# Gated delta rule and cosine feed-forward on one core: the first pair's triangular blocks inverted by doubling on TensorE, and a new order of all work

## The chip, the cores and the metric

One Trainium2 chip, one of its cores. The metric is the time of one execution in microseconds on the device, as the median over runs. The kernel's five engines are TensorE (PE), VectorE (DVE), ScalarE (ACT), GpSimd (POOL) and SyncE (SP); each takes its own instructions in the order in which they were issued to it, and they wait for each other through semaphores. Transfers are issued from SP and ACT.

## What is computed

Two blocks, one behind the other. The first is a delta-rule attention over 768 time steps for 4 batches and 8 heads of 48; the second a feed-forward block whose activation is h cos(h).

```python
k_n = k / (np.linalg.norm(k, axis=-1, keepdims=True) + 1e-06)
state = np.zeros((B, H, D, D))
for t in range(S):
    kt, vt, bt = (k_n[:, :, t], v[:, :, t], beta[:, :, t, None])
    y[:, :, t] = np.einsum('bhd,bhde->bhe', q[:, :, t], state)
    v_old = np.einsum('bhde,bhd->bhe', state, kt)
    state = state + bt[:, :, :, None] * np.einsum('bhd,bhe->bhde', kt, vt - v_old)
...
x = attn_out.transpose(0, 2, 1, 3).reshape(B * S, H * D)   # 3072 x 384
h = x @ w_in                                               # 384 x 2048
out = (h * np.cos(h)) @ w_out                              # 2048 x 384
```

## The kernel before

**Tiles.** The 768 steps are cut into 24 units of 32. The four batches lie side by side on the 128 partitions, 32 steps each. Two units make a pair, and a pair of units gives 256 tokens for the feed-forward block; there are 12 pairs.

**A unit.** k, q and v are loaded and k and q turned by PE (`turn`, L592, `turn_out`, L602). `gram` (L625) multiplies k with k and q; `gram_keys` (L636) scales the key part by beta and by the norms of k (a power on POOL, L544, task `norms`, and five small DVE operations, task `scale`), and `gram_queries` (L659) masks the other. Within a unit the recurrence is a unit lower triangular 32x32 system for each batch and head. Its matrix I + N, with N strictly triangular, is inverted once, and the unit is finished by matmuls: `state` (L795, what the state so far gives), `right` (L812), `solve` (L861 or L867, the inverse times the right side), `solve_out` (L879), `update` and `update_out` (L892, L900, the new state), `within` and `within_out` (L909, L922), and `features` (L930), which turns the result for the feed-forward block.

**The inverse of a pair** goes through memory, so that 128 partitions each hold half the rows of one of the 64 blocks of 32x32: `gram_put` writes the scaled key products, `gram_get` reads them back in the other layout (L698), `eye` puts an identity (L714), `inv` in seven pieces runs over the columns, two operations each (a product into `part`, L735, and a difference, L742), `put` writes the inverse (L756), and `get` reads it for each unit (L775). For pairs 1 to 11 this is done on POOL.

**Pair 0** is different (`HALVED = 1`). `fold` (L648 to L653) keeps the two 16x16 blocks on the diagonal and sets the block below them aside. The 16x16 blocks go the same way through memory, 15 columns, on DVE, in a bank of PSUM. Each unit of this pair then takes three steps of matmuls instead of one: `solve_half` (p_w, L825, with the half inverses), `between` (p_v, L825, with the block set aside, L845 taking the difference), and `solve`.

**The feed-forward block.** w_in and w_out come as pairs of 32-bit words, 12 and 16 transfers (`weights`, L487), and are made into 32-bit floats in three steps: `split` on ACT (L495, L497), `shift` on DVE (L501, L506) and `add` on POOL (L510). For pairs 0 and 1 `hidden(p, f)` (L951) multiplies features by w_in, 24 records of matmuls each; `hidden(0, 0)` needs blocks 0 to 2 of w_in, `hidden(0, 2)` 0 to 5, `hidden(0, 4)` 0 to 8 and `hidden(0, 6)` all 12. `turns`, `rest`, `cos` and `gate` make h cos(h) on ACT and DVE. `out` (L1148) multiplies by w_out; `out(0, 0, k)` needs its first 4k + 4 blocks. From pair 2 on the first product is made in 20 products of sums (`layer`, L1125, with `x_sum`, L1040, on DVE or POOL), and from pair 1 on the second in 7 (L1205, with `left` sums, L1221, on DVE or POOL).

**The order.** Every piece of work is a task with a key such as `('gram', 3)`. A table `LINE` lists all tasks in one order, found beforehand by a search; they are emitted in that order, so it fixes each engine's queue, and all transfers of SP and ACT are also held in that one order. A set `OTHER` names the tasks that take the other of two engines: ACT instead of SP for a transfer, POOL instead of DVE (or the reverse, for `x_sum`) for a sum.

Of the kernel before, what the change touches and what calls it, by code (L numbers as in the profile page):

```python
# [10 lines left out]
FP = mybir.dt.float32  # L11
# [5 lines left out]
C = 32  # L17
# [7 lines left out]
def _consts():  # L25
# [14 lines left out]
            p[:, None] // 16 % 2 == np.arange(2)[None, :],  # L40
# [6 lines left out]

class Order:

    OTHER = {  # L50
        ('gram_put', 0), ('put', 0), ('get', 1), ('k', 2), ('gram_put', 2), ('q', 3), ('v',
        3), ('gram_get', 1), ('k', 5), ('k', 6), ('gram_put', 6), ('get', 6), ('v', 7),
        ('gram_put', 7), ('blocks', 8, 1), ('blocks', 9, 1), ('gram_put', 9), ('blocks', 11,
        1), ('put', 5), ('get', 11), ('blocks', 12, 1), ('gram_put', 12), ('blocks', 13, 1),
        ('put', 6), ('get', 14), ('put', 7), ('v', 16), ('blocks', 16, 0), ('get', 17),
        ('k', 18), ('v', 18), ('put', 9), ('k', 20), ('gram_get', 10), ('gram_put', 22),
        ('blocks', 23, 1), ('store', 0, 1), ('right', 4, 4), ('right', 3, 4), ('left', 1, 1,
        1), ('left', 1, 4, 0), ('in_sums', 20), ('x_sum', 2, 'd'), ('x_sum', 2, 'n'),
        ('x_sum', 2, 'm'), ('x_sum', 2, 'e'), ('x_sum', 2, 'k'), ('x_sum', 2, 'g'),
        ('x_sum', 2, 'l'), ('x_sum', 2, 'f'), ('left', 2, 1, 0), ('left', 2, 2, 0), ('left',  # L60
        2, 4, 0), ('store', 2, 0), ('x_sum', 3, 'd'), ('x_sum', 3, 'n'), ('x_sum', 3, 'e'),
        ('x_sum', 3, 'k'), ('x_sum', 3, 'g'), ('x_sum', 3, 'i'), ('x_sum', 3, 'l'),
        ('x_sum', 3, 'f'), ('x_sum', 3, 'h'), ('x_sum', 3, 'b0'), ('left', 3, 2, 0),
        ('left', 3, 3, 0), ('x_sum', 4, 'd'), ('x_sum', 4, 'n'), ('x_sum', 4, 'm'),
        ('x_sum', 4, 'e'), ('x_sum', 4, 'g'), ('x_sum', 4, 'f'), ('x_sum', 4, 'h'),
        ('x_sum', 4, 'b0'), ('left', 4, 1, 0), ('left', 4, 2, 0), ('left', 4, 1, 1),
        ('store', 4, 1), ('x_sum', 5, 'd'), ('x_sum', 5, 'n'), ('x_sum', 5, 'm'), ('x_sum',
# [156 lines left out]
def kernel(  # L224
# [99 lines left out]
    nc.vector.memset(bq, 0.0)  # L324


    HALVED, HC = 1, C // 2
    off_blocks, half_zt = [], []
    eye16 = early[:, EYE : EYE + HC * HC].rearrange("p (r i) -> p r i", i=HC)
    half_tiles = [  # L330
# [1445 lines left out]
```

## Time and profile before

| | |
|---|---|
| median of 3 runs | 653.76 us (650.46, 653.76, 655.24) |
| the profiled execution: time, span | 656.46 us, 654.7 us |
| PE busy | 594.1 us (91%) |
| DVE, ACT, POOL busy | 504.0 (77%), 295.2 (45%), 457.0 (70%) |
| moved by transfers | 51.52 MB in 215,628 packets |
| granted TensorE clock, mean | 0.998 |
| chain that ended last | PE 72%, POOL 8%, DMA 8%, DVE 4%, issue 3% |

The span is the time from the first to the last instruction that the profile shows; the time of the execution is 1.8 us longer. The chain that ended last is followed back from the last instruction, at each step to what released it. A row of groups gives a line of the kernel, engine, operation, tiles and sizes, the number of records, their busy time and mean, and the idle time before them with what ended it.

### The profile page before, as it was taken

What the parts mean: (1) busy time and instruction counts of PE and PEld (TensorE: products, weight loads), DVE (VectorE), ACT (ScalarE), POOL (GpSimd) and SP (SyncE); (2) the same over time, 40 slices, a digit from 0 to 9 for tenths busy, and PEclk for the clock granted to TensorE, in tenths of its full rate; (3) what the DMA queues carried; (4) which work ended last, traced back from release to release, by engine and by line L of the source; (5) the groups of instructions that cost most, each with busy time, mean ns of one, the idle gap of its engine ahead of it and who ended that gap; (6) DMA issues with size and microseconds to landing.
All of it is one profiled execution on the core that took longest, in us unless ns stands there. A gap on an engine that the chain in (4) does not pass through costs nothing.

```text
span 654.7 us, 23397 instructions
## 1 busy us (share of the span) xinstructions
PE 594.1 (91%) x9784; PEld 555.2 (85%) x9784; DVE 504.0 (77%) x1035; ACT 295.2 (45%) x518; POOL 457.0 (70%) x813
## 2 busy tenths in 40 slices
PE   3315689999999999999999999999899999999996
PEld 3204689897899999998999999999898999999996
DVE  4684487899899987987879879889668778666581
ACT  2533365663234454634634535536334545545340
POOL 4368868978888778887788788748687388424130
PEclk9999999999999999999999999999999999999999
DMA  8886576462373363454352631441541300300000
GB/s 167 193 192 151 132 178 143 92 135 48 62 125 57 53 114 57 87 80 74 71 85 43 110 53 41 67 90 22 97 69 26 82 12 3 58 2 25 1 24 25
DMA packets 215628, 51.52 MB, mean 79 GB/s; under 512 B 207076, under 2 KB 210420, under 8 KB 215524
## 3 DMA queue, kind: packets, MB, share of 16 engines
q1 hardware_dynamic: 160168, 35.06, 28.0%
q10 hardware_dynamic: 55100, 14.53, 11.1%
q8 instruction: 77, 1.26, 0.8%
q0 software_dynamic: 256, 0.45, 0.3%
q14 instruction: 27, 0.22, 0.1%
HBM read 39.24 MB, written 10.75 MB: 76 GB/s over the span
## 4 chain that ended last, share of the span: by engine, by line
PE 72%; POOL 8%; DMA 8%; DVE 4%; issue 3%; ACTq 2%; ACT 1%; SPq 1%; POOLq 0%; DVEq 0%
PE p_out L1205 25%; PE p_h L1125 23%; PE p_h L951 7%; PE p_out L1148 3%; POOL z L742 3%; POOL part L735 3%; PE p_kq L795 3%; PE p_u L867 2%; PE p_s L892 2%; DMA gb<-g_dr 2%; PE p_kq L909 2%; DMA kp<-in_k_dram 2%; PE p_g L625 2%; PE p_h L1205 1%; PE p_z L930 1%
## 5 line engine op out<-in xcount | busy, mean ns | idle before, releaser
L735 POOL TENSOR_TENSOR part<-z,gb 128x126 f32<-128x126 f32 (+22 forms) x341 | 149.5, 439 | 53.8 <-DMA gb<-g_dr 17.7
L742 POOL TENSOR_TENSOR z<-z,part 128x126 f32<-128x126 f32 (+22 forms) x341 | 154.7, 454 | 26.7
L1205 PE MATMUL p_out<-w_out,g_ffn 128*128 128x192 f32 x672 | 121.7, 328 | 3.1 <-ACT o L1244 2.0
L1205 PEld LDWEIGHTS p_out<-w_out,g_ffn 128*128 128x128 f32 x672 | 107.8, 190 | 4.5 <-ACT o L1244 2.2
L1004 ACT ACTIVATE turns<-turns,halfpi 128x512 f32<-128x512 f32 x96 | 68.3, 720 | 82.2 <-DVE turns L995 72.1
L1205 PE MATMUL p_out<-w_sum,g_ffn 128*128 128x192 f32 x496 | 91.1, 330 | 1.4 <-DVE o L1257 1.4
L1125 PE MATMUL p_h<-x_sum,w_in 128*128 128x128 f32 x640 | 83.3, 278 | 0.2
L1205 PEld LDWEIGHTS p_out<-w_sum,g_ffn 128*128 128x128 f32 x496 | 79.4, 190 | 2.8 <-DVE o L1257 1.6
L1125 PEld LDWEIGHTS p_h<-x_sum,w_in 128*128 128x128 f32 x640 | 77.5, 191 | 1.9 <-ACT p_h L1137 0.4
L988 ACT ACTIVATE turns<-g_ffn,quarter_turn 128x512 int32<-128x512 f32 x70 | 49.6, 718 | 50.8 <-DVE g_ffn L1142 18.0
L1142 DVE TENSOR_TENSOR g_ffn<-g_ffn,p_h 128x512 f32<-128x512 f32 x80 | 54.0, 681 | 16.1 <-PE p_h L1125 15.0
L1007 DVE TENSOR_TENSOR g_ffn<-turns,g_ffn 128x512 f32<-128x512 f32 x70 | 52.0, 751 | 14.0 <-ACT turns L1004 13.7
L922 ACT COPY y<-p_kq 32x384 f32<-32x384 f32 x96 | 45.2, 470 | 36.2 <-PE p_kq L909 31.2
L995 DVE SCALAR_TENSOR_TENSOR turns<-g_ffn,turns 128x512 f32<-128x512 f32 x70 | 54.1, 781 | 7.5 <-ACT turns L988 7.3
L1125 PE MATMUL p_h<-x_sum,in_sum 128*128 128x128 f32 x400 | 53.8, 278 | 0.3 <-POOL x_sum L1040 0.2
L1125 PEld LDWEIGHTS p_h<-x_sum,in_sum 128*128 128x128 f32 x400 | 49.6, 191 | 1.7 <-POOL x_sum L1040 0.7
L951 PE MATMUL p_h<-x_ffn,w_in 128*128 128x128 f32 x384 | 48.2, 284 | 0.2 <-issue 0.2
L1221 POOL TENSOR_TENSOR g_ffn<-g_ffn 128x512 f32<-128x512 f32 x21 | 29.9, 1426 | 25.8 <-DVE g_ffn L1007 15.6
L951 PEld LDWEIGHTS p_h<-x_ffn,w_in 128*128 128x128 f32 x384 | 45.9, 198 | 1.4 <-issue 0.3
L544 POOL TENSOR_TENSOR knrm<-ksum,halves 128x16 f32<-128x16 f32 (+1 forms) x14 | 37.9, 2709 | 12.3 <-DVE ksum L532 12.1
L1257 DVE SCALAR_TENSOR_TENSOR o<-p_out,o 128x192 f32<-128x192 f32 x74 | 25.0, 351 | 27.3 <-PE p_out L1205 26.7
L1125 PE MATMUL p_h<-x_ffn,w_in 128*128 128x128 f32 x320 | 42.3, 276 | 0.0
(135 smaller groups left out, 1020.6 us busy)
## 6 DMA issues: line engine op xcount, KB each, us to landing
gb<-g_dr SPq DMA_DIRECT2D x18, 256.0 KB
g_ffn<-in_moe_w_out_dram SPq DMA_DIRECT2D x11, 384.0 KB
vp<-in_v_dram SPq DMA_DIRECT2D x80, 48.0 KB
g_ffn<-in_moe_w_in_dram SPq DMA_DIRECT2D x6, 512.0 KB
g_ffn<-in_moe_w_in_dram ACTq DMA_DIRECT2D x6, 512.0 KB
kp<-in_k_dram SPq DMA_DIRECT2D x112, 24.0 KB
out_dram<-o SPq DMA_DIRECT2D x14, 192.0 KB
zt<-z_dr SPq DMA_DIRECT2D x72, 32.0 KB
```

Of the source, the lines that this page charges most:

```text
L544: nc.gpsimd.tensor_tensor(out=scales[m][2][:, part], in0=sums[m, part.start][:, 0:n], in1=halves[:, 0:n], op=ALU.pow,)
L735: eng.tensor_tensor(out=part, in0=z[:, 0:rows, j, None].to_broadcast(shape), in1=a[:, j, None, j + 1 :].to_broadcast(shape), op=ALU.mult,)
L742: eng.tensor_tensor(out=behind, in0=behind, in1=part, op=ALU.subtract)
L922: nc.scalar.copy(by_parity(y[quarter(b)]), p_kq[quarter(b ^ 1), :, b % 2])
L951: nc.tensor.matmul(p_h[:, i], w_in[:, t, (4 * k + i) * 128 : (4 * k + i + 1) * 128], xts[p][:, t, unit * 128 : (unit + 1) * 128], start=(i ...
L988: nc.scalar.activation(turns[p, f], hidden_of(p, f), AF.Identity, bias=quarter_turn, scale=TURN)
L995: nc.vector.scalar_tensor_tensor(out=r, in0=hidden_of(p, f), scalar=TURN, in1=t, op0=ALU.mult, op1=ALU.subtract,)
L1004: nc.scalar.activation(r, r, AF.Sin, bias=halfpi, scale=2.0 * math.pi)
L1007: nc.vector.tensor_tensor(out=place(p, f), in0=step_of(rests.pop((p, f)), f), in1=step_of(hidden_of(p, f), f), op=ALU.mult,)
L1125: nc.tensor.matmul(p_h[:, e], in_block(*w)[:, e], x_of(p, b), start=new and e == 0, stop=True, skip_group_check=True,)
L1142: nc.vector.tensor_tensor(out=part_of(p, to), in0=part_of(p, one), in1=part_of(p, two), op=op)
L1205: nc.tensor.matmul(p_o, left(p, part, a)[:, e % 4], right(e, b), start=(e == 0), stop=(e == FT // 2 - 1), skip_group_check=True,)
```

## The change

Pair 0 no longer goes through memory. For its two units N is kept in place, four blocks of 32x32 on the partitions and eight heads side by side, and the inverse is made by matmuls of 32x32 blocks. First the two 16x16 blocks on the diagonal: with M their N, (I - M)(I + M^2)(I + M^4)(I + M^8) is built in four levels, of which the first squares M, the next two square and multiply at once, and the fourth only multiplies; each also carries the transpose that the next one needs as its stationary side. The last two levels put in the block below the diagonal: OFF times the inverse, then the inverse times that, which is subtracted. Each level is done for even and odd heads by themselves (`par`). The matmuls write a bank of PSUM of those that `hidden` uses; ACT copies what the next level needs, DVE makes the sums, and DVE transposes once. The powers lie in the tiles `in_sum` (unit 0) and `w_sum` (unit 1), which the feed-forward block uses later. The folds, `solve_half`, `between` and the choice of engine for `inv` are gone, and both units of pair 0 take one `solve`.

```diff
-    HALVED, HC = 1, C // 2
+    DOUBLED = 2
...
+    masks_dr = nc.inline_tensor(_masks(), name="masks")
+    masks = in_sum.rearrange("p a b c -> p (a b c)")[:, MASKS : MASKS + 3 * C]
+    nc.gpsimd.dma_start(out=masks, in_=masks_dr.ap())
+    near_block, far_block, eye32 = (masks[:, i * C : i * C + C] for i in range(3))
...
+    def double_first(n):
+        masked(n, N_T, near_block)
+        m = power(n)
+        nc.vector.transpose(m[:, N1], m[:, N_T])
+
+    def double_rest(n):
+        m = power(n)
+        nc.vector.tensor_tensor(
+            out=m[:, Y0], in0=eye32[:, None, :].to_broadcast([128, H, C]), in1=m[:, N_T],
+            op=ALU.subtract,
+        )
+        masked(n, OFF, far_block)
+        gs.pop(n)
+
+    LEVELS = [
+        [(0, N_T, slice(N1, N1 + 1)), (1, N1, slice(N_T, N_T + 1))],
+        [(1, P2, slice(P2_T, Y0 + 1)), (0, P2_T, slice(P2, P2 + 1))],
+        [(0, P4, slice(Y1, Y1 + 1)), (1, P4_T, slice(P4, P4 + 1))],
+        [(0, P8, slice(Y2, Y2 + 1))],
+        [(0, OFF, slice(Y3_T, Y3_T + 1))],
+        [(0, MIX_T, slice(Y3, Y3 + 1))],
+    ]
...
+    def double(n, level, par):
+        m = power(n)
+        p = p_ds[n, par] = h_bank("p_d", n, level, par).rearrange(
+            "p x (j i) -> p x j i", i=C
+        )
+        for at, one, two in LEVELS[level]:
+            for j in range(NP):
+                for b in range(B):
+                    nc.tensor.matmul(
+                        p[quarter(b), at : at + two.stop - two.start, j],
+                        m[quarter(b), one, 2 * j + par],
+                        m[quarter(b), two, 2 * j + par],
+                    )
+
+    def double_copy(n, level, par):
+        to, at = COPIES[level]
+        nc.scalar.copy(power(n)[:, to, par::2], p_ds[n, par][:, at])
+
+    def double_add(n, level, par):
+        m = power(n)
+        to, one, at = ADDS[level]
+        nc.vector.tensor_tensor(
+            out=m[:, to, par::2], in0=m[:, one, par::2], in1=p_ds[n, par][:, at],
+            op=ALU.subtract if level == 5 else ALU.add,
+        )
+
+    def double_turn(n, par):
+        m = power(n)
+        nc.vector.transpose(m[:, Y3_T, par::2], m[:, Y3, par::2])
...
     def solve(n):
-        zt, rhs = zts.pop(n), rhss.pop(n)
+        zt, rhs = power(n)[:, WHOLE] if n < DOUBLED else zts.pop(n), rhss.pop(n)
```

In the declaration of the tasks, the sums of `in_sum` now also wait for `solve` of both units, and the loads of k and v no longer wait for `gram_get` of pair 0. `LINE` and `OTHER` are wholly new. Read out by name, the transfers and POOL's work begin so (`w` is `weights`; the first loads of k, q, beta and constants stand ahead in both):

```text
transfers before: w0 k2 w1 k3 w2 q2 gram_put0 gram_put1 w3 q3 w4 gram_get0 v0 k4 w5 v1 w6
  gram_put2 w7 k5 gram_put3 put0 gram_get1 w8 q4 w9 get0 w10 k6 w11 get1 w12 q5 v2 w13 ...
transfers after:  w0 k2 q2 w1 k3 w2 q3 k4 w3 v0 w4 k5 gram_put2 w5 gram_put3 q4 w6 gram_get1
  v1 w7 k6 w8 v2 w9 w10 q5 k7 v3 w11 w12 k8 w13 q6 w14 gram_put4 gram_put5 w15 w16 put1 get2 ...
POOL before: norms norms norms norms add2 clear add0 add3 add5 add4 add1 norms add6 add7 inv1(3 of 7)
  add9 add8 inv1(2) add10 inv1(2) add12 add11 add13 add15 add17 norms inv2 ...
POOL after:  norms norms norms clear add0 norms add2 add3 add1 norms add4 add5 inv1(4) add6 inv1(3)
  add8 add10 add7 norms add9 add12 add11 add13 add14 add15 inv2(4) add17 add19 inv2(1)
  add16 add18 add20 inv2(2) add21 ...
```

On PE, the new order has turn(2), gram(1), turn(3), gram(2), gram(3) and turn(4) between the levels of the doubling; turn(5) ahead of features(0); and behind it the last two levels of unit 1, gram(4), hidden(0, 0), solve(1), update(1), hidden(0, 2). Of ACT's work, split(5) and split(6) stand between the copies of the later levels, and split(9) ahead of within_out(0). Of DVE's, weigh(0), which needs v of unit 1, stands ahead of the transposes of even heads of unit 0. Over the whole kernel 28 of the 110 `x_sum` operations move from DVE to POOL, and four `left` sums and one sum of w_out from POOL to DVE. The last three stores of the last pair stand together at the very end; before, one of them did.

## What the change was predicted to do

> **What bounds the kernel now.** The busy tenths of the page come first (40 slices of 16.4 us).
>
> ```profile
> PE   3315689999999999999999999999899999999996
> POOL 4368868978888778887788788748687388424130
> DMA  8886576462373363454352631441541300300000
> ```
>
> TensorE (PE) is full from the seventh slice to the end; of its idle 60.6 us (span 654.7 less 594.1 busy) 48.7 lie in the first 90 us. So the time is the moment at which PE fills up, about 91, plus some 564 us of nearly unbroken PE work. The stretches, next, say what fills instead: time, then busy us of PE, PEld, DVE, ACT, POOL, granted clock, DMA share, GB/s.
>
> ```profile
> 40.00:50.00 10.00, 1.09 (x4) 0.71 (x4) 6.51 (x8) 3.71 (x6) 9.27 (x6) 1.00 0.85 183
> 60.00:70.00 10.00, 5.51 (x167) 4.65 (x159) 8.10 (x13) 5.71 (x11) 9.06 (x16) 1.00 0.63 146
> 100.00:120.00 20.00, 20.00 (x366) 17.34 (x365) 15.99 (x31) 11.58 (x22) 17.73 (x36) 1.00 0.63 146
> 300.00:400.00 100.00, 98.76 (x1533) 94.59 (x1534) 84.22 (x173) 48.48 (x83) 80.48 (x144) 1.00 0.40 69
> ```
>
> To 50 us the transfers run at 81 to 87% of the DMA engines; from 40 to 80 POOL is 84 to 93% busy; then PE. The chain of waits in order of time names the transfers: start, us, what.
>
> ```profile
> 37.46 4.17 DMA kp<-in_k_dram
> 45.35 4.77 DMA gb<-g_dr
> 55.59 5.17 DMA w_sum<-z_dr
> 60.83 3.65 DMA g_ffn<-in_moe_w_out_dram
> ```
>
> The second is the Gram blocks of pair 1, the third the inverse of pair 0 coming back. Last the timeline (start, us, engine, line):
>
> ```profile
> 48.10 1.09 PE L592 MATMUL p_t<-consts,qp 128*128 128x128 f32 x4 [9.49 <-DMA qp<-in_q_dram]
> 50.42 0.23 POOL L735 TENSOR_TENSOR part<-z,gb 128x31 f32<-128x31 f32 x1
> 53.12 1.90 PE L825 MATMUL p_w<-vp,w_sum 32*32 32x48 f32 x64 [3.93 <-ACT kq_t L602]
> 53.98 0.32 POOL L735 TENSOR_TENSOR part<-z,gb 128x78 f32<-128x78 f32 x1
> 54.38 0.71 POOL L742 TENSOR_TENSOR z<-z,part 128x78 f32<-128x78 f32 x1
> 76.58 0.88 PE L825 MATMUL p_w<-rhs,w_sum 32*32 32x48 f32 x64
> 82.77 0.23 POOL L742 TENSOR_TENSOR z<-z,part 128x16 f32<-128x16 f32 x1
> 99.47 2.94 PE L951 MATMUL p_h<-x_ffn,w_in 128*128 128x128 f32 x24
> ```
>
> Here q of unit 4 arrives at 48.1, the inverse of pair 1 takes POOL from 50.42 to 83.0, the first solve step of unit 0 is at 53.12, and hidden(0, 8) starts at 99.47. (A matmul counts as two records: x64 is 32 matmuls.)
>
> **Transfers.** To q of unit 4 the old order issues 8.8 MB (nine blocks of w_in of 512 KB, thirteen loads of k, q and v of 192 KB, the constants, the round trips), and the stretches before 48.1 moved 8.9 MB. So arrival goes by bytes issued, and the cumulative curve (1.8, 3.6, 5.5, 7.4, 9.3, 10.8 MB at 10, 20, ... 60 us) dates the new order. To q of unit 4 it issues 6.2 MB: 34 us. Gram blocks of pair 1 (7.2 MB): 39. v of unit 1 (7.4): 40. w_in block 9 (9.4): 51. q of unit 5 (10.1): 55. This holds while SP, which now passes gram_put(3), gets there in time: my walk puts gram_keys(3) at 31, with some 1.2 MB (7 us) still in flight.
>
> **Pair 0.** Removed: 30 DVE column steps (15 x 0.204 + 15 x 0.213 = 6.3 us), the folds (six DVE operations, 1.8 us), gram_put, gram_get, put and 16 get transfers, and p_w and p_v of both units (0.9 to 1.9 us each). Added: 24 groups, 288 per unit, of 32x32 matmuls. No row shows one; p_g (32 matmuls, 64 columns) takes 1.18 early and 0.86 later, so 32 of them take between 0.8 and 1.2 and 16 half of that; I take 1.1 and 0.55, the early ends, 20 us in all, on a PE that was idle. Per level and parity come an ACT copy and a DVE add of 0.3 to 0.4 us (L712, 128x256 out of PSUM: 0.38). A level is then 1.2 to 1.9 us, six levels and the transpose about 10 us from gram_keys(0) at 13. But the copies stand in ACT's queue behind split(5) and split(6), which wait for w_in blocks, and turn(4), which waits for q of unit 4 (34), stands on PE ahead of level 4. The transpose for parity 0 stands behind weigh(0), which needs v of unit 1 (40) and takes 1.1. So: 42.3, transpose 0.3, two levels of 1.2, solve(0) ends near 46, instead of 60.2. These covers are also the limit: a level may cost 1 us more and nothing moves.
>
> **From solve(0) to PE's work.** solve_out 1.0, update 1.6, within 1.5: 50.7. within_out stands behind split(9) (51), ends near 54. features(0) stands on PE behind turn(5) (q of unit 5, 55 to 57.2): 58. With turn_out(5), features_out and gram(4) ahead, hidden(0, 0) starts near 60.5 instead of 71.5. It takes 4.9 there (1.01 + 3.93) and solve(1), update, within, hidden(0, 2) follow to about 73.
>
> **POOL decides next.** The inverse of pair 1 starts at 40 instead of 50.4. It took 32.6 us less two stretches of adds (2.56 + 1.29) = 28.7; that of pair 2, beside more DVE work, 39.2 less 8.4 of adds = 30.8. I take 29.5. With add(6) (1.3) it ends at 70.8. Behind it now stand add 8, 10, 7 (3 x 1.3: 74.7, lets hidden(0, 4) start), norms(3) 3.3, add 9, 12, 11 (3.6): 81.7, lets hidden(0, 6) start. It ends 84.6, turn(6) 1.04, and hidden(0, 8) starts at 85.7 instead of 99.5. Of the 13.8 us, 1.4 go off for solve(2), which the old order has done by then: lead 12.4.
>
> A 128x78 step took 0.71 at 54.38, while DVE ran L501 on two SBUF inputs, and 0.32 at 53.98. [...]
>
> **Given back.** out(0, 0, 1) needs add(16) and add(18), now behind five of seven pieces of pair 2's inverse. On POOL from 81.7: three adds 3.1, sixteen columns 15.8 (pair 1's, less adds), two adds 2.0, four columns 4.0, two adds 2.0 = 108.6. PE reaches it after 21.2 us of listed work from 85.7, at 106.9: 1.8 lost. At the end three stores instead of one follow the last collect, at 0.4 us of issue each: 1.0. Of the rest, 28 x_sums move from DVE (0.35) to POOL (0.65), 18 us over 500 on a POOL that is 56 to 83% busy there; four left sums and one right sum go the other way. PE idles only 4.9 us from 200 to 600, so nothing much is to be had there; I take 0.
>
> **Sum.** 12.4 - 1.8 - 1.0 = 9.6 off the span: 645.1. The profiled run was 656.46 for a span of 654.7, and the median of the three is 653.76; taken off that median: 644.2. This kernel's runs spread 0.7%, and within 1% (647.2 to 660.3) counts as no change.
>
> **Rivals.**
> 1. POOL takes the gain. If the inverse of pair 1, now beside DVE's shifts and doubling, costs what the later ones do on average (304.2/11 = 27.7 busy plus 62 gaps of 0.075 = 32.3), and its start waits for shift(5) until 43, hidden(0, 6) comes 5.8 us later: 650. For it: POOL at 9 tenths from 40 to 70. Against: pair 1 paid 28.7 beside similar work. [...] Chance 0.25.
> 2. More than forecast. If the adds overlap pauses of PE that I counted (the 1.8, and 4 us between hidden(0, 2) and hidden(0, 6)) and the new order saves half of the 4 us of PE waits that the old one has between 631 and 638, 8 us come on top: 636. Against: the new queue has the adds behind the inverse in black and white. Chance 0.15.
> 3. Slower. SP issues in order, and gram_put(3) stands ahead of q of unit 4, w_in block 6 and all that follows. It needs gram(3), which on PE stands behind five doubling groups, and these behind ACT copies that queue behind splits. Each us past 38 (31 plus the 7 in flight) empties the DMA engines and delays every later arrival. Beyond 47 the whole lead is gone; at 54 (some 25 hand-overs each 0.9 us dearer than 0.1 to 0.2) the span is 661, the time 660 to 662. For it: PE waits on such hand-overs all through the first 50 us. Against: the old order issued its own at 34.7 with 30 DVE steps in between. Chance 0.10.
> 4. That the doubling is hidden anyway: the first pair is not what held PE, but w_in. The blocks needed by hidden(0, 6) are all in by 61 in both orders, so it cannot be earlier than some 65. That leaves the forecast standing, and needs no chance of its own.
>
> **How the numbers follow.** Forecast (641 to 647): 0.50. Rival 1 (647 to 654): 0.25. Rival 2 (634 to 641): 0.15. Rival 3 (past 653): 0.10, a third of it within 1%. Faster 0.65, same 0.28, slower 0.07. The range 636 to 655 leaves out the ends of rivals 2 and 3.
>
> **What would show it.** Right: solve(0) at 44 to 48, hidden(0, 0) at 58 to 63, the inverse of pair 1 beginning at 39 to 42, hidden(0, 6) released by w_in adds at 80 to 84, PE full from 86. Wrong: gram_put of unit 3 after 38, DMA share under 0.7 between 30 and 50, hidden(0, 8) after 95, or new PE idle after 200.

## The result, and the profile after

| | before | after |
|---|---|---|
| median of 7 runs each, same chip | 653.26 us (650.46 to 655.24) | 658.6 us (656.43 to 660.87) |
| ratio, 95% interval | | 1.0082 (1.0053 to 1.0111) |
| the profiled execution: time, span | 656.46, 654.7 us | 656.43, 654.6 us |
| PE busy, records | 594.1 us, 9,784 | 609.3 us, 10,680 |

The changed kernel is 0.8% slower, where 1.5% faster was forecast; 658.6 lies above the range. In a second comparison on another chip the ratio was 1.0119 (1.0092 to 1.0146). The profiled executions are equal by chance (the one of before is slower than all its timed runs, the one of after is the fastest of its seven), so they tell places and mechanisms, and the ratios tell the time.

First the busy tenths of the changed kernel (40 slices of 16.4 us):

```profile
PE   4855878999999999999999999999999999999996
...
POOL 4368788998878678988886888886887883252340
...
DMA  9686364484434444543543442624314202100000
```

PE now has more work in the first slices, as it should with the doubling, but it is full only from the eighth slice on; before, it was from the seventh. The stretches say the same in numbers (time, then busy us of PE, PEld, DVE, ACT, POOL, granted clock, DMA share, GB/s):

```profile
40.00:50.00 10.00, 6.68 (x284) 5.68 (x276) 3.29 (x11) 4.67 (x12) 6.64 (x12) 0.50 0.91 221
60.00:70.00 10.00, 7.77 (x228) 6.69 (x222) 7.02 (x16) 3.39 (x8) 8.82 (x18) 0.50 0.37 80
100.00:120.00 20.00, 16.95 (x349) 14.99 (x348) 17.70 (x31) 12.21 (x24) 17.49 (x36) 1.00 0.45 114
300.00:400.00 100.00, 99.68 (x1744) 95.27 (x1743) 83.35 (x167) 45.78 (x80) 82.33 (x159) 1.00 0.39 69
```

Between 100 and 120 us, where PE had no gap before, 3 us are idle. Between 300 and 400 PE is fuller than before (99.7 for 98.8), which pays for part of what the start loses. The chain of waits, in order of time, has three pieces one behind the other in which nothing is awaited and no work is done, 6.1 us together (start, us, what):

```profile
32.73 1.21 issue
...
35.67 2.82 issue
...
40.42 2.07 issue
```

In the timeline of PE (start, us, engine, line, operation, records; in brackets the idle time before the group and what ended it) this "issue" is found in the middle of groups:

```profile
18.72 0.97 PE L684 MATMUL p_h<-in_sum 32*32 32x32 f32 x54 [1.49 <-issue]
...
31.98 0.75 PE L616 MATMUL p_g<-kq_t 48*32 48x64 f32 x52
33.94 0.33 PE L616 MATMUL p_g<-kq_t 48*32 48x64 f32 x12 [1.21 <-issue]
...
35.02 0.65 PE L684 MATMUL p_h<-in_sum 32*32 32x32 f32 x52
38.49 0.37 PE L684 MATMUL p_h<-in_sum 32*32 32x32 f32 x11 [2.82 <-issue]
...
42.49 0.42 PE L684 MATMUL p_h<-in_sum 32*32 32x32 f32 x12 [2.07 <-issue]
...
49.61 0.36 PE L684 MATMUL p_h<-in_sum 32*32 32x32 f32 x9
52.47 0.54 PE L684 MATMUL p_h<-in_sum 32*32 32x32 f32 x23 [2.49 <-issue]
...
56.67 1.50 PE L824 MATMUL p_u<-vp,in_sum 32*32 32x48 f32 x64 [0.41 <-DVE in_sum L697]
...
72.77 4.26 PE L914 MATMUL p_h<-x_ffn,w_in 128*128 128x128 f32 x24
...
92.83 4.02 PE L914 MATMUL p_h<-x_ffn,w_in 128*128 128x128 f32 x20 [3.34 <-POOL w_in L501]
...
97.56 2.84 PE L914 MATMUL p_h<-x_ffn,w_in 128*128 128x128 f32 x24
```

At 31.98 stand 52 of 64 Gram records, then PE stops for 1.21 us, then the other 12 follow. These wait for nothing that the profile shows: the group's waits stand ahead of its first record. Ahead of solve(0), which starts at 56.67, five such stops take 1.49 + 1.21 + 2.82 + 2.07 + 2.49 = 10.1 us. The last of them is not on the chain above, which has a transfer from 49.95 on, but it delays solve(0) too: an addition on DVE waits 3.01 us for these matmuls, until 53.07, and weigh(0), the next on DVE and ahead of the transposition that solve(0) needs, follows it without a pause (53.34). The stretches from 0 to each stop, PE alone, count the records (x) that were done:

```profile
0.00:33.94 33.94, 20.11 (x725) 1.00 0.78 163
0.00:38.49 38.49, 21.84 (x853) 0.99 0.78 169
0.00:42.49 42.49, 23.78 (x980) 0.95 0.80 175
0.00:52.47 52.47, 30.03 (x1234) 0.86 0.80 182
0.00:63.02 63.02, 36.37 (x1489) 0.80 0.78 183
```

From stop to stop that is 128, 127, 254 and 255 records: always 128 or twice 128, within two records. The table of DMA queues names what comes at that pace, in the first 100 us, before and after:

```profile
q8 instruction: 10, 0.16, 0.8%
```

```profile
q8 instruction: 17, 0.28, 1.2%
```

Seven more packets of 16.4 KB. Over the whole span the queue has 77 packets (1.26 MB) for 9,784 records before and 84 (1.38 MB) for 10,680 after, one for every 127; of weight loads the profile counts as many as of matmul records, 9,784 and 10,680. Read as one thing, the two counts (128 records from stop to stop, one packet for every 127) say that PE's instructions arrive in blocks of about 128 records, and that PE stops where 128 small matmuls are done sooner than the next block is there. The runs below test it.

On POOL, the inverse of pair 1 starts at 47.24 and hidden(0, 6) waits at 92.83 for its weight additions (the 3.34 above): the lead at hidden(0, 8), 97.56 for 99.47, is 1.9 us, 0.5 after the 1.4 for solve(2).

### The profile page after: what moved, and what is told of

It is laid out like the page before. It is cut to its first block, busy times and chain, and to the rows that moved or that the text cites. A ratio compares the mean times of both kernels' runs of the same rounds, so it can differ in the third digit from the quotient of the medians.

```text
span 654.6 us, 25186 instructions
## 1 busy us (share of the span) xinstructions
PE 609.3 (93%) x10680; PEld 570.3 (87%) x10680; DVE 501.7 (77%) x999; ACT 294.7 (45%) x530; POOL 467.4 (71%) x837
## 3 DMA queue, kind: packets, MB, share of 16 engines
q8 instruction: 84, 1.38, 0.9%
## 4 chain that ended last, share of the span: by engine, by line
PE 76%; DMA 8%; POOL 6%; DVE 3%; issue 2%; SPq 2%; ACT 1%; ACTq 0%; POOLq 0%; DVEq 0%
PE p_out L1168 27%; PE p_h L1088 26%; PE p_kq L792 3%; PE p_s L855 3%; PE p_kq L872 3%; PE p_h L914 2%; PE p_g L616 2%; POOL z L759 2%; PE p_out L1111 2%; PE p_u L830 2%; POOL part L752 2%; PE p_h L684 2%; PE p_h L1168 2%; DMA kp<-in_k_dram 1%; DMA g_ffn<-in_moe_w_in_dram 1%
## 5 line engine op out<-in xcount | busy, mean ns | idle before, releaser
L759 POOL TENSOR_TENSOR z<-z,part 128x126 f32<-128x126 f32 (+22 forms) x341 | 156.8, 460 | 26.7
L970 DVE TENSOR_TENSOR g_ffn<-turns,g_ffn 128x512 f32<-128x512 f32 x70 | 54.0, 781 | 9.8 <-ACT turns L967 9.7
L914 PE MATMUL p_h<-x_ffn,w_in 128*128 128x128 f32 x384 | 50.1, 290 | 4.0 <-POOL w_in L501 3.3
L1184 POOL TENSOR_TENSOR g_ffn<-g_ffn,g_ffn 128x512 f32<-128x512 f32 x13 | 17.9, 1379 | 37.0 <-PE p_out L1168 20.0
```

Source lines behind the costliest of these rows:

```text
L759: nc.gpsimd.tensor_tensor(out=behind, in0=behind, in1=part, op=ALU.subtract)
L914: nc.tensor.matmul(p_h[:, i], w_in[:, t, (4 * k + i) * 128 : (4 * k + i + 1) * 128], xts[p][:, t, unit * 128 : (unit + 1) * 128], start=(i ...
L970: nc.vector.tensor_tensor(out=place(p, f), in0=step_of(rests.pop((p, f)), f), in1=step_of(hidden_of(p, f), f), op=ALU.mult,)
L1184: either(("left", p, x, s), nc.vector, nc.gpsimd).tensor_tensor(out=left(p, s, to), in0=left(p, s, one), in1=left(p, s, two), op=op)
```

## The experiments

The theories: **F**, the fetch of PE's instructions; **H**, the hand-overs to copies and additions that queue behind weight splits on ACT; **D**, data that come later than the byte count says; **C**, a lower granted clock (the column shows 0.50 between 40 and 70). A matmul of 32-bit values is two records (the 32 Gram matmuls of a unit are the 64 above); the texts of the runs with three factors, with repeated Gram matmuls and with unit 1 later count it as one, so their edits were twice as many blocks as they say.

**Fewer records, more records, fewer loads.** Three factors instead of four:

```diff
-        [(0, P4, slice(Y1, Y1 + 1)), (1, P4_T, slice(P4, P4 + 1))],
-        [(0, P8, slice(Y2, Y2 + 1))],
+        [(0, P4, slice(Y1, Y1 + 1))],
+        [],
```

> Edit: in the changed kernel the fourth factor of the doubling product is left out (the eighth power and its product with the sum; the addition at that level becomes a copy), for both units; the hand-overs between TensorE, ScalarE and VectorE and the order stay. 128 matmuls fewer before the first solve step (64 per unit), which are 128 records, one in four of the blocks in which the doubling runs. Theory F (TensorE stops while its next block of instructions is fetched, because the fetch shares the 16 DMA engines with the loads): the stops stand at every 128th matmul record and there is one fewer before solve(0), four where the changed kernel had five, so solve(0) comes 1.2 to 2.8 us earlier than 56.67, plus at most 1 us for the matmuls themselves. Rival H (hand-overs to copies that stand behind the weight splits on ScalarE): the number of hand-overs is the same, the stops stay where they were or go, solve(0) within 1 us of 56.67. Time: F 1 to 4 us below the changed kernel (654 to 657), H within 1 us of it.

The eighth power's factor is left out. Measured: solve(0) at 52.06, 4.6 us earlier; three stops ahead of it (2.04, 1.73, 1.96) instead of five, and the ratio 1.0011 (0.9978 to 1.0045), against 1.0082 and 1.0119 of the changed kernel. 256 records fewer are two blocks, and the five stops' 10.1 us became 5.7, which is nearly the 4.6 won: that is F at its double size. It doesn't exclude H by itself, since the edit also takes out a copy on ACT and the addition's wait for PE, which the text counts as kept.

```diff
+        if t == 5:
+            m = power(0)[0:1, WHOLE, 0, 0:16]
+            held = dram.tile([1, 16], FP, name="held")
+            nc.sync.dma_start(out=held, in_=m)
```

> Edit: in the changed kernel, the loads of input-weight blocks 5 to 8, of k of unit 6 and of v of unit 2 are held on SyncE's queue until the inverse of unit 0 is complete (a 64-byte store of a part of that inverse is put ahead of them, which waits for its last addition); their splits, shifts and additions follow behind solve(0). The loads the first solve step needs stay ahead. Theory F: with the DMA engines nearly idle from about 43 us on, the stops at 42.5 and 52.5 (2.07 and 2.49 us) shrink below 0.7 us each, and the one at 38.5 (2.82) below 1.5; solve(0) at 50 to 53 instead of 56.67. Rival D (the data, v of unit 1 and the Gram blocks, come late): the stops inside the groups of doubling matmuls stay as long as they are, and solve(0) moves only by what v of unit 1 comes earlier. Rival C (a lower granted clock): matmul groups of the doubling stay at 0.9 to 1.1 us for 32, solve(0) within 1 us. The time of the whole is not at issue: the held weights arrive later, so all of them expect 2 to 8 us more than the changed kernel.

Here F as first put was wrong. The stops ending at 34.83, 38.28, 42.83 and 50.37 took 1.64, 1.72, 2.62 and 0.48 us, with a DMA share of 0.38, 0.56, 0.82 and 0.00 during each; solve(0) came at 54.36. Two stops of 1.7 us with the engines about half empty: a loaded DMA engine may lengthen a stop (the shortest is the one with nothing moving), but it is not what makes one. (With the weights held back the time was 671.57.)

```diff
-        for j in range(NP):
+        for j in [j for _ in range(4 if n in (2, 3) else 1) for j in range(NP)]:
```

> Edit: in the kernel before, the Gram matmuls of units 2 and 3 (32 each) are issued four times over with the same operands and results: 192 matmuls more, which are 192 records, 1.5 blocks of 128, on a TensorE that waits for data in that stage. No hand-over, copy, load or order is changed. Theory F: the kernel before now shows stops inside these groups, with nothing awaited, at its records 384 and 512 or near them, 0.5 to 3 us each while the loads run; its own stops (0.56 at 59.47, 0.24 at 72.72) move to other instructions. Rivals H, D and C: no new stop inside a group, 32 of these matmuls take 0.8 to 0.9 us each time. Time: within 2 us of the kernel before by both, since solve_half(0) has slack on TensorE.

384 records more, three blocks. The kernel before, with no doubling, now stops inside the repeated Gram groups:

```profile
25.05 2.91 PE L625 MATMUL p_g<-kq_t 48*32 48x64 f32 x191 [2.60 <-ACT kq_t L602]
29.42 1.19 PE L625 MATMUL p_g<-kq_t 48*32 48x64 f32 x65 [1.47 <-issue]
...
33.67 2.79 PE L625 MATMUL p_g<-kq_t 48*32 48x64 f32 x180 [1.16 <-ACT kq_t L602]
39.29 1.37 PE L625 MATMUL p_g<-kq_t 48*32 48x64 f32 x76 [2.83 <-issue]
```

191 + 65 and 180 + 76 are the two groups of 256; inside them PE stops for 1.47 and 2.83 us with nothing awaited. H, D and C allow no such stop. Its time was 660.92 in one run, beside a median of 657.41, which says little.

**The fetch by itself.** Late in the changed kernel, where almost nothing is transferred, the Gram matmuls of the last unit eight times over (`8 if n == 23 else 1` in the same place):

> Edit: in the changed kernel the 64 Gram matmuls of the last unit (at 495.6 us, where they take 0.86 us and the loads take a quarter of the DMA engines' time) are issued eight times over with the same operands and results, so that 512 matmuls, four blocks of 128, follow each other with nothing to wait for. It measures the fetch by itself, with little else on the DMA engines. If a block takes 3.0 to 3.5 us to fetch whatever the load (as the run with held loads says: stops of 1.64 and 1.72 with the DMA engines 4 to 43% busy, where the 128 matmuls took 1.8), the 512 take 10 to 13 us, with two to four stops of 1 to 1.7 us and nothing awaited. If the stops come from the loads only, as theory F had it, the 512 take 6.9 to 8 us with stops under 0.4. Without any limit by the fetch: 6.9 us and no stop. The time is the changed kernel's plus that.

```profile
502.17 1.91 PE L616 MATMUL p_g<-kq_t 48*32 48x64 f32 x156
506.25 1.91 PE L616 MATMUL p_g<-kq_t 48*32 48x64 f32 x128 [2.17 <-issue]
510.00 2.04 PE L616 MATMUL p_g<-kq_t 48*32 48x64 f32 x128 [1.83 <-issue]
513.74 1.70 PE L616 MATMUL p_g<-kq_t 48*32 48x64 f32 x100 [1.70 <-issue]
```

```profile
GB/s 0 0 0 0 0 0 0 0 0 0 60 0 0 0 0 0 0 0 0 0 0 0 60 0 0 0 0 0 0 0 0 0 0 0 0 60 0 0 0 0
...
q8 instruction: 3, 0.05, 1.8%
```

The 512 records take from 502.17 to 515.44, 13.27 us instead of 6.9 (8 x 0.86). A full block starts every 3.75 us (506.25, 510.00, 513.74), its 128 records are done in 1.91 to 2.04, and PE stops for the rest. The second fence has the transfer rate in 40 slices of 0.275 us: next to nothing moves but one instruction packet per block, at 507.9, 511.2 and 514.8, that is 1.1 to 1.7 us after a block has begun and 2.1 to 2.5 us before the next one does. So it is a latency, 3.75 us for each 128 records or 29 ns a record here, not a share of a loaded DMA engine. It is no fixed least: with the loads held, the blocks of the stops ending at 34.83 and 38.28 began 3.45 us apart, 27 ns a record. Where the matmuls are longer it does not show: the 128x128 matmuls of hidden take 2.94 us for 24 records (99.47 of the kernel before), by estimate 15.7 for 128, and between 300 and 400 us, with 1,744 records of 57 ns on average, PE of the changed kernel idles 0.3 us in all. The Gram records here take 1.91 us for 128, 15 ns each, and it shows at every block.

**Other orders.** Unit 1's later doubling steps behind solve(0), and the changed kernel again beside it:

```diff
-  PE:  double(0,2) double(1,2,1) ... double(1,2,0) ... double(1,3) ... double(0,5,0) solve(0) update(0) within(0) ...
+  PE:  double(0,2) ... double(0,5,0) solve(0) double(1,1) update(0) within(0) double(1,2) state(1) double(1,3) ...
```

> Edit: the changed kernel with another order only: the second to fifth steps of unit 1's doubling (matmuls, copies, additions, the transposition), which stood among those of unit 0, stand behind solve(0), within(0), state(1) and turn(5), and are still done before solve(1). Ahead of solve(0) there are 160 matmuls fewer, 1.25 blocks of 128; nothing else is taken away. Theory F: one stop fewer ahead of solve(0) (2 to 2.5 us) and 2 us of matmuls and hand-overs of unit 1 out of the way: solve(0) at 51 to 53.5 instead of 56.67, and, if unit 1's later steps fit into the waits between solve(0) and hidden(0,0), a time 2 to 5 us below the changed kernel on this chip. Rival H (the waits of unit 0's own chain of matmul, copy and addition set the time): solve(0) within 1.5 us of 56.67, time within 1.5 us of the changed kernel.

> No edit: the changed kernel once more, beside the others on the same chip, and a second profile of it. Its ratio to the kernel before was 1.0082 (1.0053 to 1.0111), so 1.005 to 1.011 again. The profile shows by how much the stops vary from one execution to another: theory F expects them at the same matmul records (124 to 128 apart) as in the first profile, five ahead of solve(0) of 1 to 3 us each, whatever the execution.

The second profile of the changed kernel has its stops at the same groups, 1.66, 1.91, 2.20, 2.07 and 1.41 ahead of solve(0) (57.74); the ratio was 1.0119. With unit 1 later, solve(0) came at 55.79 only, since a copy on ACT held PE for 5.97 us, and the stops moved behind it (1.67, 0.47, 4.75, 0.73): hidden(0, 0) at 82.03 and 1.0175 (1.0124 to 1.0226). The stops went with the records; moving them was no remedy here.

**The order without the doubling.** The kernel before to 210 us, then to 290 us, and the changed kernel's order behind it:

```diff
+  LINE = the old LINE to ('collect', 1, 3)   (second run: to ('left', 2, 3, 0)), then the other tasks as the new LINE has them
+  OTHER = the old one for the tasks of the first part, the new one for the rest
```

> Edit: the kernel before (its inverse of pair 0 in two halves, no doubling) with its own order and choices of engines and queues for the first 576 of its tasks (to about 210 us), and the order and choices of the changed kernel for all work behind that. It tells the two parts of the change apart. If the newly searched order is better behind the start, as the idle time of TensorE says (between 200 and 640 us 5.3 us in the kernel before, 1.1 in the changed one, and 1.1 us less work in the last 15), the time is 4 to 5 us below the kernel before (648 to 650), and the loss of the changed kernel lies wholly ahead of 200 us. If that gain is what a late start gave (work that waits leaves fewer holes behind it), the time is within 1.5 us of the kernel before.

> Edit: as the first merged kernel (the kernel before with its own order at the start, the changed kernel's order behind it, no doubling), but joined later, at the 752nd task (about 290 us), where the two orders differ by 7 tasks and not by 9. In the first one the join itself cost up to 4.4 us of TensorE's time between 210 and 240 us. If the new order is worth what the idle time says (behind 290 us: 5.0 us idle in the kernel before, 1.1 in the changed one), and the join costs less than 1 us: 2 to 4 us below the kernel before. If the orders are worth the same: within 1.5 us of it.

Ratios 1.0000 (0.9966 to 1.0035) and 1.0028 (0.9995 to 1.0061). Both profiles show PE waits at or ahead of the join (4.4 us between 200 and 240 in the first, 3.3 us for an x_sum at 271.84 in the second), so what the new order is worth by itself stays open; joined like this it gives 0.3% at the most (the lower ends of the intervals).

**Fewer records with all products kept.** The second product of three steps replaced by transpositions, then that in another order:

```diff
-        [(0, N_T, slice(N1, N1 + 1)), (1, N1, slice(N_T, N_T + 1))],
-        [(1, P2, slice(P2_T, Y0 + 1)), (0, P2_T, slice(P2, P2 + 1))],
-        [(0, P4, slice(Y1, Y1 + 1)), (1, P4_T, slice(P4, P4 + 1))],
+        [(0, N_T, slice(N1, N1 + 1))],
+        [(1, P2, slice(P2_T, Y0 + 1))],
+        [(1, P4, slice(P4_T, Y1 + 1))],
...
+    FLIPS = {0: (P2_T, 0), 1: (P4, 1), 2: (P8, 1)}
+        nc.vector.transpose(power(n)[:, to, par::2], p_ds[n, par][:, at])
```

> Edit: in the changed kernel the second product of steps 0, 1 and 2 of the doubling, which only gives the other orientation of the power, is replaced by one transposition on VectorE straight from the result (12 transpositions for both units); the third step's two products become one of double width. The result is the same inverse. Ahead of solve(0) there are 192 matmuls fewer, and since the trace has two records for each matmul of the program, 384 records, three blocks of 128. Theory F in its new form (a block takes 3.74 us to fetch whatever else runs): up to 11 us fewer on TensorE; turn(4) waits for q of unit 4 until about 44.7 as it did with three factors, and two blocks are left behind it, so solve(0) at 50 to 52.5 instead of 56.67 or 57.74; time 4 to 8 us below the changed kernel, 0.996 to 1.003 of the kernel before. Rival H (the hand-overs set the time): six transpositions more stand in unit 0's chain, so solve(0) at 56 or later, and the time that of the changed kernel or above.

> Edit: as the run with transpositions, and in another order: the third to fifth steps of both halves of unit 0 stand next to each other, ahead of turn(4) and of weight split and shift 5; unit 1's step 2 of one half stands behind them, its step 3 behind solve(0). It tells what is left of the loss to the order of hand-overs once the records are fewer. Theory F with what the order costs besides: solve(0) at 46.5 to 49.5, bounded then by v of unit 1; unit 1's 128 records that move behind solve(0) are fetched while TensorE waits for VectorE; hidden(0,0) at 64 to 68 instead of 72.77; time 1 to 4 us below the run with transpositions, 0.992 to 1.000 of the kernel before. If turn(4), later here, holds back norms, inverse or the loads behind it: solve(0) as said, but no gain in time against the other run.

Three blocks fewer gave 1.0029 (1.0005 to 1.0053): a gain over the changed kernel, and a time that F allowed; but solve(0) came at 55.95, which is H's mark (56) and not F's (50 to 52.5). Two stops are left ahead of it (1.26 and 1.69), and a new wait stands in its place. On ACT (ACTq are the transfers it issues):

```profile
46.45 3.27 ACTq L373 DMA_DIRECT2D kp<-in_k_dram  x4
49.82 0.27 ACT L695 COPY in_sum<-p_h 128x128 f32<-128x128 f32 x1 [6.01 <-DMA kp<-in_k_dram]
```

The copy of step 4 stands behind four loads of k of unit 6, whose issue holds ACT's queue from 46.45 to 49.72. That is H, uncovered once most of the stops were gone. The other order brought solve(0) to 52.97, but put off the inverse of pair 1 to 53.24, behind a weight addition that POOL had waited 8.51 us for, and the ratio was 1.0065 (1.0037 to 1.0092).

The same with that queue cleared, and the queue alone:

```diff
-  SP:  gram_put(3) q4 gram_get(1) v1 ...                ACT: square split(4) ... split(5) eye(1) ... split(6) turn_out(4)
+  SP:  gram_put(3) gram_get(1) q4 v1 w6 w7 k6 ...       ACT: square eye(1) split(4) ... split(5) ... turn_out(4) split(6)
-  OTHER: ('k', 6), ('weights', 6), ('weights', 7)
```

> Edit: as the run with transpositions, and in the stretch from 35 to 50 us the queues are rearranged: k of unit 6 (four loads, whose issue held ScalarE's queue from 46.45 to 49.72 in that run while the copy of step 4 of unit 0 waited behind it) goes to SyncE's queue, as do weight blocks 6 and 7, all behind v of unit 1; the Gram blocks of pair 1 are fetched ahead of q of unit 4; the identity for the inverse of pair 1 is copied ahead of weight split 4, and split 6 stands behind the copy of turn(4). Nothing else is changed. Theory: with the fetch stops gone the next thing late was ScalarE's queue, so solve(0) at 51 to 53 (55.95 there), the inverse of pair 1 starts at 43 to 46 (48.65), hidden(0,0) at 66 to 68.5 (70.39), 0.993 to 1.000 of the kernel before, and below the run with transpositions by 2 us or more. If solve(0) and the inverse come earlier but the time does not, the chain behind them (weight additions on GpSimd, out(0,0,1)) sets it.

> Edit: the same rearrangement of the queues alone, in the changed kernel, without the transpositions, so with all its 1152 records of doubling. Theory F: the stops are still there, five ahead of solve(0), 1 to 3 us each; solve(0) at 54 to 57, no more than 2 us better than the changed kernel, 1.003 to 1.010 of the kernel before. If the queue of ScalarE was the cause and the stops only filled time in which TensorE would have waited: solve(0) at 51 to 53 as in the other run, and 1.000 or below.

1.0041 (1.0005 to 1.0077), no better than with the transpositions alone, and 1.0063 (1.0018 to 1.0109). With transpositions the copy went at 45.75, and now PE stopped for 3.37 us at a block's edge; solve(0) came at 55.59. Fetch and queue lay over each other, and taking away one showed the other. In the run of the queue alone the stops were all there (2.11, 2.46, 1.89, 1.80, 0.94, 2.53) and solve(0) came at 58.96, later than either theory had it.

**The changed kernel without the fetch.** Two matmuls of 128x128 with the identity in place of 16 of 32x32. The products are left out, so this kernel does not compute the inverse; it keeps the copies, additions, waits, loads and the order:

```diff
-            for j in range(NP):
-                for b in range(B):
-                    nc.tensor.matmul(
-                        p[quarter(b), at : at + two.stop - two.start, j],
...
+            for x in (slice(one, one + 1), two):
+                nc.tensor.matmul(p[:, at : at + x.stop - x.start], ident, m[:, x, par::2])
```

> Edit: in the changed kernel every product of the doubling (16 matmuls of 32x32 blocks for one half of the heads) is replaced by two matmuls of 128x128 with the identity, which read the same operands and write the same result tile: the products are left out, so the inverse of pair 0 is not computed; every copy, addition, transposition, wait, load and the order stay. 1152 records become 144, so the doubling needs about one block of instructions instead of nine, and its matmuls take about as long (two of 0.2 to 0.27 us for 16 of 0.55). It is the changed kernel as the prediction saw it, with no price on the instruction fetch. If the fetch is the cause and what was forecast behind it is right: no stop ahead of solve(0) but the first, solve(0) at 46 to 51, hidden(0,0) at 60 to 65, hidden(0,8) at 86 to 92 and 0.985 to 0.992 of the kernel before. If the chain of the Gram blocks, the inverse of pair 1 and the weight additions on GpSimd sets the end anyway: solve(0) as early, but the inverse starts at 44 or later, hidden(0,6) still waits for an addition until 90 or later, and 0.995 to 1.003 of the kernel before.

> Edit: as the run with few records, with the queues rearranged as in the two runs with free queues (k of unit 6 and weight blocks 6 and 7 on SyncE behind v of unit 1, the Gram blocks of pair 1 fetched ahead of q of unit 4, the identity and split 6 moved). The products of the doubling are left out here too. It tells whether, without the fetch, ScalarE's queue is the next thing late. If so: solve(0) 2 us or more ahead of the run with few records, at 44 to 48, and 1 to 3 us less time. If the inverse of pair 1 and the weight additions are next: the same time within 1.5 us, whatever solve(0) does.

Ratio 0.9900 (0.9865 to 0.9936). No stop is left ahead of solve(0), and from hidden(0, 0) on the forecast's dates come out within 1 to 3 us:

```profile
49.20 0.88 PE L819 MATMUL p_u<-vp,in_sum 32*32 32x48 f32 x64 [0.38 <-DVE in_sum L692]
...
61.83 2.94 PE L909 MATMUL p_h<-x_ffn,w_in 128*128 128x128 f32 x24
...
77.92 4.48 PE L909 MATMUL p_h<-x_ffn,w_in 128*128 128x128 f32 x22 [5.31 <-POOL w_in L501]
...
83.73 3.35 PE L909 MATMUL p_h<-x_ffn,w_in 128*128 128x128 f32 x24
...
87.79 2.84 PE L909 MATMUL p_h<-x_ffn,w_in 128*128 128x128 f32 x24
...
99.05 0.86 PE L616 MATMUL p_g<-kq_t 48*32 48x64 f32 x64 [1.20 <-ACT x_ffn L896]
...
101.55 2.94 PE L909 MATMUL p_h<-x_ffn,w_in 128*128 128x128 f32 x24 [0.56 <-DVE g_ffn L965]
...
113.13 2.98 PE L1106 MATMUL p_out<-w_out,g_ffn 128*128 128x384 f32 x8 [1.25 <-POOL w_out L501]
```

solve(0) at 49.20, hidden(0, 0) at 61.83, hidden(0, 6) at 83.73, hidden(0, 8) at 87.79, where 85.7 was forecast. hidden(0, 4) still waits 5.31 us for a weight addition on POOL, but that wait ends at 77.92 (74.7 forecast), and hidden(0, 6) waits for none; the second theory had it waiting until 90. Part of the gain is not the stops: PE is also faster in this run (64 solve records in 0.88 us for 1.50, hidden(0, 0) in 2.94 for 4.26). With the queues cleared too the ratio was 0.9912 (0.9884 to 0.9941), the same; solve(0) came later there (54.23), as turn(4), ahead of it on PE, waited 4.81 us for q of unit 4. So ACT's queue is not the next thing late.

**Half the records, all products.** The powers as 16-bit floats (the operands are rounded, the completed inverse is in 32 bits):

```diff
+HALF = mybir.dt.float16
...
-        return whole[:, 0 : POWERS * H * C].rearrange("p (x h i) -> p x h i", h=H, i=C)
+        whole = whole.bitcast(HALF)[:, 0 : POWERS * H * C]
+        return whole.rearrange("p (x h i) -> p x h i", h=H, i=C)
...
-            out=m[:, to, par::2], in0=m[:, one, par::2], in1=p_ds[n, par][:, at],
+            out=(inverse_of(n) if level == 5 else m[:, to])[:, par::2],
+            in0=m[:, one, par::2], in1=p_ds[n, par][:, at],
```

> Edit: in the changed kernel the powers and sums of the doubling are held as 16-bit floats (11 bits of mantissa), the completed inverse again in 32 bits; order, hand-overs and the number of matmuls stay. A matmul of 32-bit values is two records in the trace, so one of 16-bit values should be one: 576 records for the doubling instead of 1152, four and a half blocks fewer. The operands are rounded, so the inverse is good to three or four digits. Theory F: with half the records solve(0) comes at 49 to 53 (49.20 with few records, 56.67 with all), one or two stops are left ahead of it, and the time is 0.990 to 0.998 of the kernel before, between the run with few records (0.990) and the runs with three blocks fewer (1.003). If the count of records does not halve, or the fetch goes by bytes of operands: as the changed kernel, 1.008 to 1.012.

> Edit: as the run with 16-bit powers, with the rearranged queues of the runs before (k of unit 6 and weight blocks 6 and 7 on SyncE behind v of unit 1, and the rest). With few records the queues made no difference in time (0.9912 beside 0.9900), since GpSimd's weight additions hold hidden(0,6) either way. Expected: within 0.3% of the run with 16-bit powers, in 0.989 to 0.999 of the kernel before; if ScalarE's queue does matter with stops left, 0.3 to 0.6% below it.

0.9917 (0.9885 to 0.9949), median 650.92 beside 656.55; with the queues cleared 0.9914 (0.9886 to 0.9942). The same matmuls in the same order and places, 10,104 records instead of 10,680, so the 576 matmuls of the doubling are one record each:

```profile
19.71 0.64 PE L617 MATMUL p_g<-kq_t 48*32 48x64 f32 x22 [2.68 <-issue]
...
35.33 0.27 PE L691 MATMUL p_h<-w_sum 32*32 32x32 f16 x11 [1.19 <-issue]
...
48.48 1.77 PE L832 MATMUL p_u<-vp,in_sum 32*32 32x48 f32 x64 [0.41 <-DVE in_sum L704]
...
65.15 3.98 PE L922 MATMUL p_h<-x_ffn,w_in 128*128 128x128 f32 x24
...
91.85 2.84 PE L922 MATMUL p_h<-x_ffn,w_in 128*128 128x128 f32 x24
```

Two stops of over a microsecond (2.68 and 1.19) are left ahead of solve(0), which starts at 48.48, 8.2 us earlier. Stops took 4.3 us there with one of 0.47, for 10.1; the rest is less work, since PE is busy 598.9 us for 609.3. The solve records are as slow as in the changed kernel (1.77 for 1.50), so little of this gain is a faster PE. By the ratios this kernel is faster than the one before and than the changed one.

## Why the prediction was wrong

**The step that failed** is the price of the doubling: "20 us in all, on a PE that was idle", and with it the margin, "a level may cost 1 us more and nothing moves". The 1.1 us for 32 matmuls is what a group takes once its instructions are there (1.06 to 1.08 in the trace after, for the groups without a double width). What it left out is the fetch, a term that the sum doesn't have: 1152 records are nine blocks, by estimate 9 x 3.75 = 33.8 us. The idle engine was counted as free, and no price was put on its instruction stream. In the changed kernel 10.1 us of it show as stops ahead of solve(0); the rest passes beside PE's own work and its other waits. The sign of it was in the profile of before, where p_u of unit 0 is cut in two (the row of p_v above it is used further down):

```profile
55.65 1.50 PE L825 MATMUL p_v<-g_ffn,w_sum 32*32 32x48 f32 x64 [0.62 <-ACT g_ffn L837]
57.90 1.01 PE L861 MATMUL p_u<-g_ffn,w_sum 32*32 32x48 f32 x39 [0.75 <-DVE g_ffn L845]
59.47 0.71 PE L861 MATMUL p_u<-g_ffn,w_sum 32*32 32x48 f32 x25 [0.56 <-issue]
```

39 records, a stop of 0.56 us with "issue", and 25 records more make the 64 of one group, and 77 packets on the instruction queue for 9,784 records give the block. That the fetch is the cause is shown by three kinds of run: records added where they should have cost nothing (stops appear), records issued by themselves (3.75 us a block), and records taken away with order, copies and waits kept (0.9900 and 0.9917).

**Transfers by bytes.** Right within 2 us for the Gram blocks and some 6 us too early for q, and up to 6 for v, even without the fetch. With few records gram_put(3) was issued at 32.09 (gram_keys(3) forecast for 31) and the inverse of pair 1 began at 41.85 (40 forecast); but turn(4) waited for q of unit 4 until 39.71 (34), and weigh(0), which needs v of unit 1, ran at 45.84 (40), straight behind an addition. SP issued this q at 32.58, behind gram_put(3), and it was there 7 us later: a count of the bytes issued leaves out when the queue gets to issue them. In the changed kernel, two stops lie ahead of gram_put(3), and it was issued at 34.80. Without the fetch solve(0) ended 4 us later than forecast (50.1 for 46), for which the error in q and v is the likely reason, and hidden(0, 8) 2 us later. So of the 12 us by which solve(0) ended late in the changed kernel (58.17), some 8 go when the records go and 4 stay.

**From solve(0) to hidden(0, 0).** 46 to 60.5 was forecast, 14.5 us; 58.17 to 72.77 in the changed kernel is 14.6. That is partly luck: a stop of 0.62 and a slower PE lie in it, and with few records it is 11.7 (50.08 to 61.83).

**POOL.** The length of pair 1's inverse was right (29.5 forecast, 30.8 with add(6) in it; 47.24 to 77.46, with that addition, is 30.2), so rival 1 is out as it was put: the inverse was late, but not longer. Its start was not (40; 47.24): the Gram blocks were late by the stops, and the copy of the identity stood on ACT behind doubling copies that waited for PE. With 16-bit powers it starts at 42.50. The two 128x78 steps that the prediction sets side by side are a product (0.32, L735) and a difference (0.71, L742). The same difference took 0.34 at 79.15, where DVE ran L845 from 79.07, and 0.71 at 54.38, where DVE ran L501 and, from 54.82, L506: twice the time beside these two (one of 128x81 took 0.34 at 53.56, with DVE idle). What in them does it, and whether it grows with DVE's load, no run shows; the forecast's 29.5 doesn't use it.

**hidden(0, 6) and (0, 8).** hidden(0, 6) was released by an addition, as forecast, at 92.83 instead of 80 to 84; with few records it started at 83.73 with no such wait. The chain was right, and its start 12 us late.

**Given back.** 1.8 us forecast for out(0, 0, 1). Measured with few records: 1.20 + 0.56 + 1.25 in the lines above, and 1.45 + 1.07 at 135.58 and 136.93 for an inverse coming back, 5.5 us together, 3.7 more than forecast. With hidden(0, 8) 2 us late this is more than the 3 us by which that run's gain fell short (6.6 us of 657.6, and 9.6 forecast); what won the rest back wasn't traced. In the changed kernel PE idles 5.2 us between 100 and 160. On the other side, the order behind 200 us was taken at 0 and PE idles 1.0 us instead of 4.9 from 200 to 600: that and the shorter tail (8.4 us of PE work behind 640 us for 9.6) bring the profiled span level with before.

**Rivals.** Rival 3 had the sign and a wrong reason: gram_put(3) was 34.8, far from its 47, and the DMA share stayed at 0.91 from 40 to 50. Of the marks that were to show the forecast wrong, hidden(0, 8) after 95 came true. C fell: with 0.50 granted in the changed kernel 64 solve records took 1.50 us at 56.67, and p_v of before took 1.50 at 55.65 with 1.00 in that column. The runs say the same: with transpositions the column shows 1.00 from 40 to 70 and solve(0) still came at 55.95; with 16-bit powers it shows 1.00 too and the solve records are no faster.

Open: the worth of the new order without the doubling, how much of the gain with few records is PE's faster pace, and the doubling with block-diagonal operands, which would keep 32 bits and by the count of blocks (four on the 128 partitions) need a quarter of the matmuls; it wasn't tried.

## What to carry to other kernels

Count instructions as well as microseconds: in these runs small matmuls came at 27 to 29 ns a record at best once the blocks ran out, where the matmuls alone took 15, so look twice at a stage that has several hundred records and less than 3.75 us for each 128. Here fewer records helped (16-bit operands, and in part transpositions elsewhere), and another order or held loads did not. In a profile, look for groups broken in the middle with nothing awaited, and count the records between the breaks. Where one fix leaves the time where it was, look at what now stands at the same place: here the stops and a queue on ACT lay over each other, and only runs that took half of the records or more away showed the gain behind them.

## What was not expected of the hardware

With the DMA engines empty, PE's instructions came in blocks 3.75 us apart, one packet for each, 1.1 to 1.7 us after the block before it had begun. When PE asks for a block, no run shows. In the changed kernel, with the engines at some 80%, stops were 1.2 to 2.8 us, and 1.7 to 2.2 with the engines empty at 506 us, so the loads matter less than the latency. And the column of the granted clock does not tell the pace of a group by itself: the two rows of 64 records in 1.50 us above stand beside 0.50 and 1.00.
